# Output products, weight sums and bank copies moved around at the boundary between two layers

## The chip, the cores and the metric

The kernel runs on one core of a Trainium2 chip. The metric is the time of one execution in microseconds; the time before is the median of three runs.

## What is computed

Rotary attention on 2 x 8 heads of 576 tokens, then two feed-forward layers on the 1152 token rows, all with results to float32 accuracy (products run as pairs of hi and lo halves):

```python
attn = softmax(rotate(q) @ rotate(k).T / 8) @ v          # 16 heads, 576 x 64
x = attn as [1152, 512]
h = x @ w_in;   g = where(h > 0, h, exp(h) - 1);  x = g @ w_out    # 512 -> 2048 -> 512
h = x @ w2_in;  g = h * tanh(softplus(h));        out = g @ w2_out # 512 -> 2048 -> 512
```

## The kernel before

Every engine has one queue that it works through in order. Inside a `manual_schedule` block (L1311 to L1335) the order of the program is the order of each queue, so the code is the schedule.

A float32 matrix is split into a hi half (rounded by ScalarE) and a lo half (the rest, a subtract on VectorE or GpSimd), and a product takes three passes: hi by hi, hi by lo, lo by hi. Raw weights come from memory by DMA on SP's queue into three rotating buffers; ScalarE converts them (`rebase`, L92), VectorE restores their bits in three passes (`bits`, L103, L107, L111), after which the raw buffer is free for the next DMA, and `round_weight` makes the halves: hi on ScalarE (L116), lo on GpSimd or, where `by` says so, on VectorE (L117).

The first layer ends with four times `g2_mm` (TensorE, L922), `g2_y` (the sum into Y on VectorE, L936, and XH on ScalarE, L938) and `g2_xl` (XL on VectorE, L942). XH and XL hold the halves of the second layer's input.

The second layer (`second`, L1255) treats its 16 column blocks of 128 in eight pairs. Pair 0 is done plainly: three classic units (`classic`, L207 on TensorE, one for each 384 tokens), each followed by the Mish activation (`classic_act`, L1103), the hi half (`classic_hi`, L1106) and the lo half (`classic_lo`, L1110). Pairs 1 to 7 use Strassen-Winograd's scheme with seven products (`Pair.mm`, L1044) on 288-column blocks instead of eight. It wants sums of the inputs, t1 to t4 (`form`, L886 on VectorE; `put_hi`, L909 on ScalarE; `put_lo`, L913 on VectorE), and of the weights (`Pieces.sums`, L820 on VectorE; `Pieces.round`). t1's halves are written into XH and XL in place of the input block that they replace. The products accumulate in three PSUM banks of results, a, b and c; between products `copy` (L1064, ScalarE), `add` (L1068) and `add22` (L1072, VectorE) take partial results out, and `act` (L1082, L1083) and `lo` (L1086) make the activations' halves in a tile gg.

The output of a pair is nine products, one for each 128 tokens: `out_mm` (L1122, six matmuls on TensorE, into one of two banks ps_h) and `out_sum`, which for pair 0 copies the bank to Y (L1130, VectorE) and for later pairs adds it (L1132). In the step of pair q (`pair_step`, L1136) TensorE interleaves the seven products of pair q with the nine output products of pair q - 1, while the weights of pair q + 1 (`Pieces`) and the output weights of pair q (`Block`) are prepared. `ahead_pieces` are the weights of pair 1, which the first layer's last units load.

Of the kernel before, what the change touches and what calls it, by code (L numbers as in the profile page):

```python
# [13 lines left out]
AF = mybir.ActivationFunctionType  # L14
# [11 lines left out]
def kernel(  # L26
# [11 lines left out]
    nc = tc.nc  # L38
# [4 lines left out]
    NT, DM = out.shape  # L43
# [807 lines left out]
    def moe(mp, early):  # L851
# [46 lines left out]
        def put_hi(u, name):  # L898
            if name == "t1":
                home = x_home(top, u, 1)  # L900
            else:
                if u == 0 and name != "t4":
                    t = main.tile([128, 2, 2 * CH], F32R, tag="ge", name="ge", bufs=GE)[:, :, 0:2 * H2]
                else:
                    t = second_pool[0].tile([128, 2, 2 * H2], F32R, name=f"x{name}{u}")
                v = t.rearrange("p i (c n) -> p i c n", c=2)
                home = v[:, 0], v[:, 1]
            XO[u][name] = home
            nc.scalar.activation(out=home[0], in_=T[u][name], func=AF.Copy)  # L909

        def put_lo(u, name):
            hi, lo = XO[u][name]
            nc.vector.tensor_tensor(out=lo, in0=T[u][name], in1=plain(hi), op=ALU.subtract)  # L913
# [30 lines left out]
        def g2_first(g, t, ep):  # L944
            g2_y(g, t, ep, g2_mm(g, t, ep))
            if g == NG - 1:
                g2_xl(t, ep)

        UB = GF // 2
        pend = []  # L950
# [3 lines left out]
        ahead_pieces = Pieces(1)  # L954
# [171 lines left out]
        def out_sum():  # L1126
            pair, t, o = banks.pop(0)
            y = Y.rearrange("p (t e) -> p t e", e=DM)[:, t, :]
            if pair.q == 0:
                nc.vector.tensor_copy(out=y, in_=o)  # L1130
            else:
                nc.vector.tensor_tensor(out=y, in0=y, in1=o, op=ALU.add)  # L1132
                if pair.q == NF // 2 - 1:
                    nc.sync.dma_start(out=out[t * 128:t * 128 + 128, :], in_=y)

        def pair_step(x, prev, w, o, on):  # L1136
            x.mm(1)
# [117 lines left out]
        def second():  # L1255
            NQ = NF // 2
            x = Pair(0)
            w = ahead_pieces
            x.classic(0)
            w.round(0)  # L1260
            put_hi(0, "t4")
            form(1, "t3")
            form(1, "t2")
            x.classic_act(0)
            x.classic_hi(0)
            x.classic(1)
            w.sums(0, 1, 2)
            w.round(2)
            put_hi(1, "t2")
            x.classic_lo(0)  # L1270
            put_lo(1, "t2")
            x.classic_act(1)
            x.classic_hi(1)
            w.sums(3)
            form(0, "t1")
            form(1, "t1")
            put_hi(1, "t3")
            x.classic(2)
            x.classic_lo(1)
            w.round(1)  # L1280
            put_lo(1, "t3")
            form(1, "t4")
            put_lo(0, "t4")
            w.round(3)
            x.classic_act(2)
            x.classic_hi(2)
            put_hi(0, "t1")
            put_hi(1, "t1")
            put_lo(0, "t1")
            put_lo(1, "t1")  # L1290
            put_hi(1, "t4")
            o = [Block(NF + 2 + j) for j in range(2)]
            for b in o:
                b.load()
            put_lo(1, "t4")
            for q in range(1, NQ):
                prev, x = x, Pair(q)
                queue.extend((prev, t) for t in range(NT // 128))
                if q + 1 < NQ:
                    on = [Block(NF + 2 * q + 2 + j) for j in range(2)]  # L1300
                    pair_step(x, prev, Pieces(q + 1), o, on)
                    o = on
                else:
                    last_step(x, prev, o)
            queue.extend((x, t) for t in range(NT // 128))
            while queue:
                out_mm()
                out_sum()

        psum("ps_g")  # L1310
        with tc.manual_schedule():  # L1311
            for n in range(len(units)):
                step(n)
            (_, g, t, ep), = pend[:1]
            pend.pop(0)
            g2_first(g, t, ep)
            warm = mp.tile([128, 1], F32, name="warm")
            nc.gpsimd.memset(warm, 0.0)
            nc.scalar.activation(out=warm, in_=warm, func=AF.Mish)
            form(0, "t3")  # L1320
            form(0, "t2")
            form(0, "t4")
            put_hi(0, "t3")
            put_hi(0, "t2")
            o = [(x[1:], g2_mm(*x[1:])) for x in pend[:1]]
            g2_y(*o[0][0], o[0][1])
            put_lo(0, "t3")
            put_lo(0, "t2")
            g2_xl(*o[0][0][1:])
            g2_first(*pend[1][1:])  # L1330
            firsts.close()
            with tc.tile_pool(name="mp2", bufs=1, reuse_waits="tile") as mp2:
                second_pool[0] = mp2
                psum("ps_h")
                second()  # L1335
# [90 lines left out]
```

## Times and profile before

| | us |
|---|---|
| median of 3 runs | 553.16 (552.18 to 553.47) |
| the profiled execution, its own time | 551.88 |
| its span, first to last instruction | 550.1 |
| TensorE busy | 537.2 |
| VectorE busy | 431.4 |
| ScalarE busy | 310.0 |
| GpSimd busy | 233.4 |
| mean granted TensorE clock | 0.999 of 2.4 GHz |

The rows below come from the profiled execution. PE is TensorE, DVE VectorE, ACT ScalarE, POOL GpSimd, SPq SP's queue. A timeline row is start in us, duration in us, engine, line, operation, output<-input by the program's names, shape and count; in brackets stands how long the engine was idle before it and what ended that idle time. Rows of a timeline that follow each other on one engine may overlap by a tenth.

### The profile page before, as it was taken

The page shows a single profiled execution, that of the slowest core. Times are in us where ns is not written, and L with a number is a line of the kernel's source. Part 1 is how long each engine was busy: PE and PEld are TensorE (multiplying, and loading weights), DVE is VectorE, ACT ScalarE, POOL GpSimd, SP SyncE. Part 2 cuts the span into 40 slices and gives each one's busy share as a digit, 9 for nine tenths or more (in the row PEclk, how much of TensorE's full clock was granted, in tenths as well). Part 3 has the DMA queues.
Part 4 walks back from the last instruction along what each step waited for, and adds up shares of the span by engine and source line. Part 5 has one row for each costly group of instructions (what it writes and reads, how often), then busy time and mean ns, then how long its engine had stood idle before and what let it go on. Part 6 is the DMA issues. An engine that isn't in the chain of part 4 may idle for free.

```text
span 550.1 us, 9065 instructions
## 1 busy us (share of the span) xinstructions
PE 537.2 (98%) x3390; PEld 488.2 (89%) x3390; DVE 431.4 (78%) x671; ACT 310.0 (56%) x548; POOL 233.4 (42%) x207
## 2 busy tenths in 40 slices
PE   7999999999999999999999999979999999999997
PEld 6678887888899999999999999978889899888985
DVE  4667776788877987988888768899788888878853
ACT  3657676678556666455455554565654645556420
POOL 6899998843415442544344211132423313141200
PEclk9999999999999999999999999999999999999999
DMA  8278878874322333223232221104132231421004
GB/s 249 95 194 222 197 212 222 207 168 122 120 86 77 116 116 113 78 82 110 77 115 77 77 77 39 39 0 154 46 108 77 76 120 35 153 75 41 1 0 173
DMA packets 49100, 59.81 MB, mean 109 GB/s; under 512 B 20768, under 2 KB 38944, under 8 KB 48288
## 3 DMA queue, kind: packets, MB, share of 16 engines
q1 hardware_dynamic: 48512, 58.64, 36.4%
q8 instruction: 27, 0.44, 0.3%
q10 hardware_dynamic: 544, 0.59, 0.3%
q14 instruction: 17, 0.14, 0.1%
HBM read 47.51 MB, written 2.36 MB: 91 GB/s over the span
## 4 chain that ended last, share of the span: by engine, by line
PE 80%; DVE 9%; ACT 3%; POOL 3%; issue 2%; DMA 2%; SPq 0%; ACTq 0%; POOLq 0%; DVEq 0%
PE ps_h L1122 18%; PE ps_s L207 17%; PE ps_g L922 14%; PE ps_s L1044 13%; PE ps_s L441 7%; PE psA L548 6%; PE psT L508 4%; DMA tab<-in_rope_dram 1%; DVE Y L936 1%; DVE gg L886 1%; DVE mn L448 1%; DVE wu L111 1%; ACT XH L938 1%; DVE XL L942 1%; DMA qb<-ql 1%
## 5 line engine op out<-in xcount | busy, mean ns | idle before, releaser
L448 DVE TENSOR_REDUCE mn<-ps_s 128x1 f32<-128x576 f32 x72 | 53.7, 754 | 25.0 <-PE ps_s L441 24.9
L1132 DVE TENSOR_TENSOR Y<-Y,ps_h 128x512 f32<-128x512 f32 x63 | 43.2, 686 | 27.8 <-PE ps_h L1122 27.5
L461 ACT ACTIVATE P<-ps_s,mn 128x576 f32<-128x576 f32 x72 | 53.0, 737 | 14.4 <-DVE mn L448 14.1
L1122 PE MATMUL ps_h<-wo0h,gg 128*128 128x512 f32 x144 | 45.3, 396 | 0.6 <-DVE Y L1130 0.6
L1122 PE MATMUL ps_h<-wo0bh,gg 128*128 128x512 f32 x144 | 45.2, 395 | 0.0
L1064 ACT ACTIVATE ta<-ps_s 128x576 f32<-128x576 f32 x28 | 18.3, 652 | 46.3 <-PE ps_s L1044 46.3
L508 PE MATMUL psT<-idn,P 128*128 128x128 f32 x288 | 43.0, 274 | 0.0
L107 DVE SCALAR_TENSOR_TENSOR wu<-raw,wu 128x512 int32<-128x512 int32 x50 | 40.2, 805 | 1.4
L117 POOL TENSOR_TENSOR wo0l<-wu,wo0h 128x512 fp32r<-128x512 f32 x12 | 17.5, 1469 | 50.8 <-ACT wo0h L116 50.8
L528 ACT ACTIVATE pt<-psT 128x512 f32<-128x512 f32 x43 | 25.5, 594 | 22.7 <-PE psT L508 22.6
L111 DVE SCALAR_TENSOR_TENSOR wu<-raw,wu 128x512 int32<-128x512 int32 x50 | 36.2, 724 | 1.5
L254 DVE SCALAR_TENSOR_TENSOR tb<-ta,tb 128x768 f32<-128x768 f32 x22 | 21.4, 975 | 20.2 <-ACT tb L250 20.1
L117 POOL TENSOR_TENSOR wo0bl<-wu,wo0bh 128x512 fp32r<-128x512 f32 x12 | 17.1, 1443 | 46.5 <-ACT wo0bh L116 40.3
L548 PE MATMUL psA<-pt,v_t 128*64 128x256 f32 (+1 forms) x240 | 36.1, 401 | 0.6 <-ACT R L493 0.3
L508 PEld LDWEIGHTS psT<-idn,P 128*128 128x128 f32 x288 | 34.7, 141 | 1.9 <-issue 1.5
L103 DVE TENSOR_SCALAR wu<-wu 128x512 int32<-128x512 int32 x50 | 31.9, 649 | 0.0
L1122 PEld LDWEIGHTS ps_h<-wo0h,gg 128*128 128x128 f32 x144 | 26.0, 188 | 6.0 <-DVE Y L1130 1.0
L1122 PEld LDWEIGHTS ps_h<-wo0bh,gg 128*128 128x128 f32 x144 | 26.4, 188 | 5.5
L207 PE MATMUL ps_s<-XH,wi0h 128*128 128x384 f32 x120 | 31.0, 338 | 0.0
L207 PE MATMUL ps_s<-XL,wi0h 128*128 128x384 f32 x120 | 30.6, 335 | 0.0
L207 PE MATMUL ps_s<-XH,wi0l 128*128 128x384 f32 x120 | 30.5, 335 | 0.0
L117 POOL TENSOR_TENSOR wi0l<-wu,wi0h 128x512 fp32r<-128x512 f32 x10 | 14.9, 1493 | 35.7 <-ACT wi0h L116 35.7
(229 smaller groups left out, 1622.8 us busy)
## 6 DMA issues: line engine op xcount, KB each, us to landing
raw<-in_w_in_dram SPq DMA_DIRECT2D x32, 512.0 KB, 3.7
raw<-in_w_out_dram SPq DMA_DIRECT2D x32, 512.0 KB, 3.3
qk_t<-in_qk_dram SPq DMA_DIRECT2D x6, 1152.0 KB, 5.4
qa<-qh SPq DMA_DIRECT2D x24, 144.0 KB, 3.4
out_dram<-Y SPq DMA_DIRECT2D x9, 256.0 KB, 2.0
ka<-kh SPq DMA_DIRECT2D x12, 144.0 KB, 5.4
ka<-kl SPq DMA_DIRECT2D x12, 144.0 KB, 5.0
qb<-ql SPq DMA_DIRECT2D x12, 144.0 KB, 3.3
```

The source lines that it names most:

```text
L107: nc.vector.scalar_tensor_tensor(out=ui, in0=high, scalar=-0x80000000, in1=ui, op0=ALU.bitwise_and, op1=ALU.bitwise_or)
L111: nc.vector.scalar_tensor_tensor(out=ui, in0=low, scalar=29, in1=ui, op0=ALU.logical_shift_right, op1=ALU.bitwise_or)
L117: (by or nc.gpsimd).tensor_tensor(out=lo, in0=u, in1=plain(hi), op=ALU.subtract)
L207: nc.tensor.matmul(o[:, j, :CH], lhsT=ws[j][i][:, cc, :], rhs=x[:, cc, t * CH:t * CH + CH], start=(k == 0), stop=(k == 3 * NC - 1),)
L448: nc.vector.tensor_reduce(out=m, in_=psS[u][:, :, :HS], axis=AX.XY, op=ALU.min)
L461: nc.scalar.activation(out=P.rearrange("p (j n) -> p j n", j=2), in_=psS.pop(u)[:, :, :HS], func=AF.Exp, scale=-1.0, bias=mn_t.pop(u), acc ...
L508: nc.tensor.transpose(tv[:, c, :], P[:, k:k + 128], idn)
L548: nc.tensor.matmul(o[64 * h:64 * h + 64, cols], lhsT=v, rhs=rhs, start=(c == 0 and first), stop=(c == 4), skip_group_check=True,)
L922: nc.tensor.matmul(o[:, j, :CH], lhsT=WO[f][w][:, e * 128:e * 128 + 128], rhs=g_part(f, t, i), start=(k == 0), stop=(k == 3 * GF - 1),)
L1044: nc.tensor.matmul(self.o[r][:, u, :H2], lhsT=w[i][:, cc, :], rhs=XO[u][xn][x][:, cc, :], start=(first and n == 0), stop=(last and n == 3 ...
L1122: nc.tensor.matmul(o, lhsT=l, rhs=w, start=(k == 0), stop=(k == 5))
L1132: nc.vector.tensor_tensor(out=y, in0=y, in1=o, op=ALU.add)
```

## The change

`out_sum` of pair 0 goes from VectorE to ScalarE. The step of pair 1 has its own function, `first_step`. Three of its nine output products are issued in `second`, between the classic units and the first pair product, together with three sums. Around these, `second` is put in another order: `w.round`, `form` and the halves come in another sequence, and t4 of the second half of the tokens is formed in `first_step`. The four weight sums go from `second` to the end of the first layer, in between `g2_y` and `g2_xl`, and the first weight rounding and the load of the Mish table come ahead of them. In `first_step` the lo halves of the second output block and of three of the four weight roundings are subtracted on VectorE (in `pair_step`: of one).

```diff
--- before.py
+++ after.py
@@ -1127,11 +1127,75 @@
             pair, t, o = banks.pop(0)
             y = Y.rearrange("p (t e) -> p t e", e=DM)[:, t, :]
             if pair.q == 0:
-                nc.vector.tensor_copy(out=y, in_=o)
+                nc.scalar.activation(out=y, in_=o, func=AF.Copy)
             else:
                 nc.vector.tensor_tensor(out=y, in0=y, in1=o, op=ALU.add)
                 if pair.q == NF // 2 - 1:
                     nc.sync.dma_start(out=out[t * 128:t * 128 + 128, :], in_=y)
+
+        def first_step(x, prev, w, o, on):
+            o[0].bits(0)
+            x.mm(1)
+            x.copy("m1", "a")
+            o[0].bits(1)
+            x.mm(2)
+            o[0].bits(2)
+            o[0].round()
+            w.load(0)
+            form(1, "t4")
+            put_hi(1, "t4")
+            put_lo(1, "t4")
+            x.mm(6)
+            x.copy("u2", "a")
+            x.add("m1", "b")
+            x.mm(5)
+            x.mm(7)
+            out_mm()
+            o[1].bits(0)
+            out_mm()
+            x.copy("m5", "c")
+            x.act("m1")
+            w.bits(0, 0)
+            out_mm()
+            w.load(1)
+            out_mm()
+            o[1].bits(1)
+            x.copy("u3", "a")
+            x.mm(4)
+            o[1].bits(2)
+            x.add22()
+            out_sum()
+            w.bits(1, 0)
+            w.bits(0, 1)
+            w.bits(0, 2)
+            w.bits(1, 1)
+            out_mm()
+            out_sum()
+            o[1].round(nc.vector)
+            out_sum()
+            x.mm(3)
+            x.act("u3")
+            w.bits(1, 2)
+            out_sum()
+            w.sums(0)
+            out_mm()
+            w.sums(1)
+            on[0].load()
+            w.sums(2)
+            w.sums(3)
+            x.act("s")
+            x.lo("u3")
+            w.round(2, nc.vector)
+            x.add("u2", "c")
+            x.lo("m1")
+            w.round(0)
+            w.round(3, nc.vector)
+            on[1].load()
+            w.round(1, nc.vector)
+            x.act("u2")
+            out_sum()
+            out_sum()
+            x.lo("u2")
 
         def pair_step(x, prev, w, o, on):
             x.mm(1)
@@ -1256,49 +1320,52 @@
             NQ = NF // 2
             x = Pair(0)
             w = ahead_pieces
+            queue.extend((x, t) for t in range(NT // 128))
             x.classic(0)
-            w.round(0)
-            put_hi(0, "t4")
+            x.classic_act(0)
             form(1, "t3")
             form(1, "t2")
-            x.classic_act(0)
             x.classic_hi(0)
             x.classic(1)
-            w.sums(0, 1, 2)
             w.round(2)
+            put_hi(0, "t4")
+            x.classic_lo(0)
             put_hi(1, "t2")
-            x.classic_lo(0)
             put_lo(1, "t2")
+            w.round(1)
+            form(0, "t1")
+            form(1, "t1")
             x.classic_act(1)
             x.classic_hi(1)
-            w.sums(3)
-            form(0, "t1")
-            form(1, "t1")
+            put_lo(0, "t4")
+            x.classic(2)
+            w.round(3)
             put_hi(1, "t3")
-            x.classic(2)
             x.classic_lo(1)
-            w.round(1)
             put_lo(1, "t3")
-            form(1, "t4")
-            put_lo(0, "t4")
-            w.round(3)
-            x.classic_act(2)
-            x.classic_hi(2)
-            put_hi(0, "t1")
-            put_hi(1, "t1")
-            put_lo(0, "t1")
-            put_lo(1, "t1")
-            put_hi(1, "t4")
             o = [Block(NF + 2 + j) for j in range(2)]
             for b in o:
                 b.load()
-            put_lo(1, "t4")
+            out_mm()
+            out_mm()
+            put_hi(0, "t1")
+            put_hi(1, "t1")
+            x.classic_act(2)
+            out_sum()
+            x.classic_hi(2)
+            out_mm()
+            out_sum()
+            put_lo(0, "t1")
+            put_lo(1, "t1")
+            x.classic_lo(2)
+            out_sum()
             for q in range(1, NQ):
                 prev, x = x, Pair(q)
-                queue.extend((prev, t) for t in range(NT // 128))
+                if q > 1:
+                    queue.extend((prev, t) for t in range(NT // 128))
                 if q + 1 < NQ:
                     on = [Block(NF + 2 * q + 2 + j) for j in range(2)]
-                    pair_step(x, prev, Pieces(q + 1), o, on)
+                    (pair_step if q > 1 else first_step)(x, prev, Pieces(q + 1), o, on)
                     o = on
                 else:
                     last_step(x, prev, o)
@@ -1313,10 +1380,14 @@
                 step(n)
             (_, g, t, ep), = pend[:1]
             pend.pop(0)
-            g2_first(g, t, ep)
+            w = ahead_pieces
             warm = mp.tile([128, 1], F32, name="warm")
             nc.gpsimd.memset(warm, 0.0)
             nc.scalar.activation(out=warm, in_=warm, func=AF.Mish)
+            w.round(0)
+            g2_y(g, t, ep, g2_mm(g, t, ep))
+            w.sums(0, 1)
+            g2_xl(t, ep)
             form(0, "t3")
             form(0, "t2")
             form(0, "t4")
@@ -1327,7 +1398,10 @@
             put_lo(0, "t3")
             put_lo(0, "t2")
             g2_xl(*o[0][0][1:])
-            g2_first(*pend[1][1:])
+            g, t, ep = pend[1][1:]
+            g2_y(g, t, ep, g2_mm(g, t, ep))
+            w.sums(2, 3)
+            g2_xl(t, ep)
             firsts.close()
             with tc.tile_pool(name="mp2", bufs=1, reuse_waits="tile") as mp2:
                 second_pool[0] = mp2
```

## Rows read from the trace of the kernel before

**Rows 1.** The page: busy us (share of the span), instructions.
```profile
PE 537.2 (98%) x3390; PEld 488.2 (89%) x3390; DVE 431.4 (78%) x671; ACT 310.0 (56%) x548; POOL 233.4 (42%) x207
```

**Rows 2.** Waits of TensorE after 150 us: total, times, longest.
```profile
PE ps_s L1044 <- ACT ta L1064: 3.3, 1, 3.3
PE ps_h L1122 <- DVE Y L1130: 0.6, 1, 0.6
```

**Rows 3.** Stretches: length, busy us (instructions) by engine, clock, DMA share, GB/s.
```profile
363.17:391.23 28.06, 24.23 (x139) 21.21 (x139) 25.23 (x39) 18.02 (x30) 9.54 (x7) 1.00 0.24 76
391.23:414.96 23.73, 23.73 (x140) 21.27 (x139) 19.43 (x34) 13.11 (x22) 6.85 (x6) 1.00 0.28 89
414.96:438.60 23.64, 23.64 (x139) 21.23 (x138) 19.33 (x34) 13.13 (x22) 6.75 (x6) 1.00 0.28 89
```

**Rows 4.** Timeline, TensorE: start, us, instruction, idle before and its releaser.
```profile
363.17 0.42 PE L1044 MATMUL ps_s<-XH,wi1h 128*128 128x288 f32 x2
...
369.75 0.40 PE L1044 MATMUL ps_s<-ge,wi1h 128*128 128x288 f32 x1 [3.26 <-ACT ta L1064]
...
371.44 0.63 PE L1122 MATMUL ps_h<-wo0h,gg 128*128 128x512 f32 x2
...
372.84 0.63 PE L1122 MATMUL ps_h<-wo0h,gg 128*128 128x512 f32 x2
```

**Rows 5.** Timeline, ScalarE.
```profile
345.42 0.85 ACT L938 ACTIVATE XH<-Y 128x768 fp32r<-128x768 f32 x1 [3.36 <-DVE Y L936]
...
346.28 1.28 ACT L1319 ACT_TABLE_LOAD   x1
...
355.32 0.79 ACT L1103 ACTIVATE ta<-ps_s 128x768 f32<-128x768 f32 x1
...
367.36 0.68 ACT L909 ACTIVATE xt<-gg 128x576 fp32r<-128x576 f32 x1 [1.15 <-DVE gg L886]
...
367.95 1.21 ACT L92 ACTIVATE wu<-raw 128x512 f32<-128x512 f32 x2
...
369.06 0.63 ACT L1064 ACTIVATE ta<-ps_s 128x576 f32<-128x576 f32 x1
...
371.64 0.65 ACT L1064 ACTIVATE ta<-ps_s 128x576 f32<-128x576 f32 x1 [1.94 <-PE ps_s L1044]
```

**Rows 6.** Timeline, VectorE and, at 354.92, GpSimd.
```profile
346.30 0.96 DVE L942 TENSOR_TENSOR XL<-Y,XH 128x768 fp32r<-128x768 f32 x1 [0.92 <-ACT XH L938]
...
354.92 1.55 POOL L117 TENSOR_TENSOR wi1l<-wv,wi1h 128x512 fp32r<-128x512 f32 x1 [18.52 <-ACT wi1h L116]
...
355.23 1.85 DVE L886 TENSOR_TENSOR gg<-Y 128x576 f32<-128x576 f32 x1
...
357.80 0.42 DVE L820 TENSOR_TENSOR ws<-wv 128x256 f32<-128x256 f32 x1
...
366.58 0.74 DVE L886 TENSOR_TENSOR gg<-Y,gg 128x576 f32<-128x576 f32 x1
...
373.63 0.69 DVE L111 SCALAR_TENSOR_TENSOR wu<-raw,wu 128x512 int32<-128x512 int32 x1
```

**Rows 7.** Groups by line, ScalarE: busy us, mean ns, idle before.
```profile
L528 ACT ACTIVATE pt<-psT 128x512 f32<-128x512 f32 x43 | 25.5, 594 | 22.7 <-PE psT L508 22.6
...
L1083 ACT ACTIVATE gg<-ta 128x576 fp32r<-128x576 f32 x21 | 14.4, 688 | 0.7
...
L92 ACT ACTIVATE wv<-raw 128x512 f32<-128x512 f32 x14 | 9.3, 666 | 5.3 <-DMA raw<-in_w_in_dram 5.3
...
L116 ACT ACTIVATE wi1h<-wv 128x512 fp32r<-128x512 f32 x8 | 4.9, 616 | 0.0
```

**Rows 8.** One line each, L1130, L117, L78: ns or us, min/median/max.
```profile
L1130 DVE COPY Y<-ps_h x9: 678/690/690, 374.2 to 391.4; 128x512 f32<-128x512 f32 x9
...
L117 POOL TENSOR_TENSOR wi1l<-wu,wi1h x8: 1287/1414/2077, 175.6 to 275.2; 128x512 fp32r<-128x512 f32 x8
...
DMA to landing us min/median/max: 3.6/3.7/7.5
```

## The prediction, made before the changed kernel was run

> **What bounds the kernel.** I read the shares of the engines first. TensorE is busy for 537.2 of 550.1 us [rows 1], so time comes back only where TensorE stands still. Next come TensorE's own waits after 150 us. There are two, 3.3 us for ScalarE's copy at L1064 and 0.6 us for VectorE's copy at L1130 [rows 2], both in the first pair step of the second layer. The table by stretch shows what they are worth: from the end of the classic units to the next step's first product this step takes 28.06 us, while the next two, with the same nine output products and seven pair products, take 23.73 and 23.64 [rows 3]. **The most that this change can return is therefore 28.06 - 23.73 = 4.33 us.**
>
> Why TensorE waits is read from the queues. Pair product 6 starts at 369.75 [rows 4] because bank a must be copied first. That copy is issued at 369.06, behind the hi half of the last input sum t4, which waits 1.15 us for VectorE, and behind two conversions of raw weights [rows 5]. VectorE forms t4 only at 366.58 [rows 6]: it is busy 25.23 of the 28.06 us [rows 3]. The second wait is for the first of VectorE's copies of an output bank; there are two such banks, and the third product needs it.
>
> **The change, part by part.**
>
> *Three output products ahead of the pair products.* Nothing is added. An output product takes 372.84 - 371.44 = 1.40 us [rows 4], and a pair product (23.73 - 9 x 1.40) / 7 = 1.59. The classic units end at 363.17 [rows 4], so without a wait the order is: outputs 1 to 3 at 363.17, 364.57, 365.97; pair products 1, 2, 6, 5, 7 at 367.4, 369.0, 370.5, 372.1, 373.7; outputs 4 to 7 from 375.3; pair product 4 at 380.9; output 8; pair product 3 at 383.9; output 9; the next step at 386.9. What could keep TensorE from this order is costed next.
>
> *The nine first sums on ScalarE.* VectorE loses nine copies of 0.69 us [rows 8], 6.2 us. ScalarE gains nine. No row shows this copy there; the nearest are its 128x512 copy out of PSUM at 0.594 [rows 7] and a 128x768 activation out of PSUM at 0.79 [rows 5]. I take 0.59, the same shape and type, and keep 0.79 as the upper end; being the shape itself, it leaves no reason for less. By the rows ScalarE is the quicker of the two for this copy. A rule of the Trainium skill speaks against this part: "ScalarE: Activation LUTs", Rules for kernel authors, sends simple elementwise work to VectorE, at up to about three times ScalarE's speed in bf16. By that page a sum would cost some 2 us (an estimate: three times 0.69), which is the case of rival C.
>
> *Weight sums in the first layer.* Two of the four VectorE passes go into the wait for ScalarE ahead of L942 at 346.30, 0.92 us [rows 6], and two into the like wait ahead of the last L942. A pass takes 0.42 [rows 6], so two fill 0.84. The first two share their place with the GpSimd subtract of the first rounding, so I add up to 0.2 us; classic 1, which waits for it, begins only when classic 0 is done, about 355 [rows 5], and hides it. Without that cover it costs 0.2.
>
> *Table load earlier, t4 later.* The load, 1.28 us, moves into a wait of 3.36 us at 345.42 [rows 5] and costs nothing; without that wait it costs 1.28. t4 is used last by pair product 4, at 380.9, and is ready about 372.
>
> *Subtracts.* Three move from GpSimd to VectorE at 0.69 [rows 6], 2.1 us more. In return fewer collide: beside a GpSimd subtract begun at 354.92 a VectorE pass took 1.85 us, the like pass alone 0.74 [rows 6]. VectorE's balance in this step is 25.2 - 6.2 + 2.1 = 21.1 us, under 23.7.
>
> *Walk through ScalarE's queue*, with the durations of [rows 5, 7], less the 0.1 by which neighbours overlap (two conversions take 1.21), a TensorE result being read 0.2 us after the next product's start (371.64 against 371.44 [rows 4, 5]). Classic 0 is activated at about 355.1. To 362.9 follow its hi half, three roundings, three input sums' hi halves, classic 1, and the two raw conversions. The hi halves of both t1 follow to 364.1; the second overwrites inputs of classic 2 and must wait until 363.4 anyway. Then classic 2's activation to 364.8 and sum 1 to 365.4. **Output 3 wants it at 365.97: cover 0.5.** Bank a is copied from 369.2 to 369.8, 0.7 ahead of pair product 6; the second copy ends at 373.0, 0.7 ahead of pair product 7. Then m5's copy, two activations of m1, a conversion and u3's copy bring sum 4 to 377.5, 0.5 ahead of output 6, and sum 5 to 378.9, 0.5 ahead of output 7. The step's end is the fullest place: pair product 3 ends at 385.6, VectorE adds u2 to 386.4, ScalarE does two activations, sums 8 and 9, and the next step's first copy to 389.4, wanted at 390.0.
>
> *VectorE.* Ahead of output 3 its last duty is the second t1: from 355.4 there are six passes, 4.7 us, and two GpSimd subtracts of 1.4 [rows 8] may hold it, so 362.9 at the latest, 0.5 before it is needed. In the next step its eleven passes from the u2 sum to the raw bits take from 386.4 to about 392.9; the output bank that it reads next is ready at 393.2, and TensorE loses time only if VectorE is more than 0.7 late there.
>
> *DMA.* The loads keep their order on SP's queue. The second weight piece is fetched once the first block's bits are done, now about 369.1, and lands 3.7 us later [rows 8], at 373; it is converted at 375.8. The next two have 3.0 and 1.9 us of cover. The worst landing, 7.5 us, would put the first 0.8 us late, 0.5 of it covered.
>
> **Sum.** All covers hold by the rows, though six of them are only 0.5 to 0.7 us. The gain is 4.33, less 0.1 for what one of these may leak: 4.2 us. After this step TensorE has no wait [rows 2], so the gain reaches the end whole: the span goes from 550.1 to 545.9. The profiled execution took 551.88, its span and 1.8 around it, and lies 1.3 below the median of 553.16. The forecast is 553.16 - 4.2 = 549.0. Its own range, with a gain of 3.8 to 4.4 and the 1 us by which medians can move, is 548.0 to 550.0.
>
> **Rivals.** *A, part of the gain leaks through the thin covers.* A GpSimd subtract has reached 2.08 us, against a median of 1.41 [rows 8]. With two such ahead of the second t1, sum 1 comes 0.8 to 1.3 late and TensorE loses 0.3 to 0.8 there; the like lateness in VectorE's string at the next step costs another 1 to 2. For it: VectorE has hardly a gap in this step [rows 3]. Against: the median would not do it. A gain of 1.1 to 3.8, about 2.5: 550.7.
>
> *B, the wait only changes its name.* A raw weight that lands late, or dependences by whole tiles, takes the place of the old 3.3 us. For it: the conversion of weight pieces waits 5.3 us in all for its DMA [rows 7]. Against: on this path it would need a landing near 11 us; and pair product 1 starts at 363.17 [rows 4] although the t1 halves, which precede it in the program and go into the tile it reads, are written after it, so dependences go by regions. About 553.
>
> *C, slower: ScalarE becomes the bound.* With nine sums it is busy some 22 of 23.7 us. Up to the next step's first copy it still idles 4.7 us in the walk, always for a TensorE result (0.8 before sum 3, 1.0, 0.85 and 0.95 before the copies of m1, u2 and m5, 0.8 and 0.3 before sums 5 and 6). The sums may grow by 4.7 / 9 = 0.5 each before that is used up; each further 0.1 costs 0.9, so the gain of 4.3 is gone at 0.59 + 0.5 + 0.5 = 1.6 us a sum, and at 2.0 the kernel is 3.6 us slower: 556.8. For it: one queue holds the bank copies, the sums and the activations in a fixed order. Against: no ScalarE pass in the rows, up to 768 columns, takes over 0.85.
>
> **Chances.** Forecast 0.64, A 0.23, B 0.07, C 0.06. The range reaches over most of A, and below by the spread of the three runs (552.18 to 553.47): 547.5 to 551.5. Faster by over 0.2% (1.1 us, about what a measurement of this kernel can tell from no change) has forecast and A, 0.87; within 0.2% B, 0.07; slower C, 0.06.
>
> **What would show it.** The stretch from the end of the classic units to the next step's first matmul should read 23.7 to 24.1 instead of 28.06, with no TensorE wait above 0.3. A sum on ScalarE should take 0.59, the six covers should stand in the order above, and nothing on TensorE should wait for t4. A TensorE wait at output 3, 6 or 7 for a sum, or a copy at L1064 much later than 0.2 us after its product, makes A right; a wait for a DMA in this step's conversions makes B right; a ScalarE without gaps from 363 to 389, and sums far over 0.6, C. The prediction is wrong at its root if the stretch is short and the span is not: then later steps give the time back.

## The result and the profile after

The changed kernel takes 547.08 us (median of four executions, 547.00 to 547.33), the kernel before 553.32 beside it (four, 552.18 to 553.94): ratio 0.989, interval 0.9873 to 0.9907. It is faster by 6.2 us, where 4.2 was forecast, and the time lies 0.4 below the lower end of the range. Those four executions of before lie high: against the 60 further ones used below (median 552.55) the change is worth 5.5.

The profiled execution took 547.04, its span is 545.3, its mean granted clock 1.0. The page's shares of the engines answer to [rows 1]:

```profile
PE 536.4 (98%) x3390; PEld 488.3 (90%) x3390; DVE 426.8 (78%) x665; ACT 314.3 (58%) x557; POOL 229.2 (42%) x204
```

TensorE's work is the same; what is gone from the span is standing still. The boundary step by stretches (length, busy us by engine with instructions, clock, DMA share, GB/s), which answers to the first line of [rows 3]:

```profile
362.68:386.39 23.71, 23.71 (x139) 21.27 (x139) 18.13 (x31) 18.79 (x33) 2.59 (x2) 1.00 0.27 89
```

The step now takes 23.71 us, as long as the two steps behind it did before, and TensorE is busy in all of it. Its list of waits has no line behind 150 us, where [rows 2] had two. The waits that are left, over the whole span (total, times, longest), are all in the attention; the three longest groups:

```profile
PE ps_s L441 <- ACT P L461: 1.9, 4, 0.7
PE psA L612 <- DVE bl L596: 1.5, 1, 1.5
PE ps_s L441 <- DVE kh L323: 0.6, 1, 0.6
```

The places where TensorE could have waited, by its timeline (start, us, instruction), answering to [rows 4]: output 1, output 3, pair product 6, pair product 7, outputs 6 and 7, the next step's first product and its product 6.

```profile
362.68 0.63 PE L1122 MATMUL ps_h<-wo0h,gg 128*128 128x512 f32 x2
...
365.47 0.63 PE L1122 MATMUL ps_h<-wo0h,gg 128*128 128x512 f32 x2
...
370.03 0.29 PE L1044 MATMUL ps_s<-ge,wi1h 128*128 128x288 f32 x1
...
373.22 0.29 PE L1044 MATMUL ps_s<-ge,wi1h 128*128 128x288 f32 x1
...
377.61 0.63 PE L1122 MATMUL ps_h<-wo0h,gg 128*128 128x512 f32 x2
...
379.00 0.63 PE L1122 MATMUL ps_h<-wo0h,gg 128*128 128x512 f32 x2
...
386.39 0.42 PE L1044 MATMUL ps_s<-XH,wi0h 128*128 128x288 f32 x2
...
389.56 0.29 PE L1044 MATMUL ps_s<-ge,wi0h 128*128 128x288 f32 x1
```

None has a bracket. What each of them needs, by ScalarE's timeline (answering to [rows 5]):

```profile
364.27 0.60 ACT L1130 ACTIVATE Y<-ps_h 128x512 f32<-128x512 f32 x1
...
368.65 0.65 ACT L1064 ACTIVATE ta<-ps_s 128x576 f32<-128x576 f32 x1 [0.98 <-PE ps_s L1044]
...
371.82 0.65 ACT L1064 ACTIVATE ta<-ps_s 128x576 f32<-128x576 f32 x1 [0.88 <-PE ps_s L1044]
...
376.40 0.60 ACT L1130 ACTIVATE Y<-ps_h 128x512 f32<-128x512 f32 x1
377.81 0.60 ACT L1130 ACTIVATE Y<-ps_h 128x512 f32<-128x512 f32 x1 [0.80 <-PE ps_h L1122]
...
388.25 0.66 ACT L1064 ACTIVATE ta<-ps_s 128x576 f32<-128x576 f32 x1
```

Start plus duration against the start in TensorE's rows gives the six covers:

| what | ends | wanted | cover | cover forecast |
|---|---|---|---|---|
| sum 1, output 3 | 364.87 | 365.47 | 0.60 | 0.5 |
| copy of m1, product 6 | 369.30 | 370.03 | 0.73 | 0.7 |
| copy of u2, product 7 | 372.47 | 373.22 | 0.75 | 0.7 |
| sum 4, output 6 | 377.00 | 377.61 | 0.61 | 0.5 |
| sum 5, output 7 | 378.41 | 379.00 | 0.59 | 0.5 |
| next step's copy, its product 6 | 388.91 | 389.56 | 0.65 | 0.6 |

So the step did what the walk said, to a tenth. The 2 us by which the forecast missed must lie elsewhere. The difference of the two profiled executions is 551.88 - 547.04 = 4.84: 28.06 - 23.71 = 4.35 in the step, and 0.49 because the classic units end at 362.68 instead of 363.17 [rows 4]. The 0.49 is not the change's doing. It is there at the first layer's first matmul, some 200 us ahead of the first instruction that was moved (the kernel before, then the changed one):

```profile
145.46 0.62 PE L207 MATMUL ps_s<-XH,wi0h 128*128 128x384 f32 x2
```

```profile
144.93 0.62 PE L207 MATMUL ps_s<-XH,wi0h 128*128 128x384 f32 x2
```

From there to the end of the classic units pass 217.71 and 217.75 us, and 217.69 to 217.77 in all fourteen traces of this case. The earlier start comes out of the attention, where nothing was changed, and the moves at the end of the first layer gain nothing ahead of the step. The medians are 6.1 to 6.2 apart. What is left, some 1.3 us, is in no part of the profiled execution of before.

### The profile page after: what moved, and what is told of

It is laid out like the page before. It is cut to its first block, busy times and chain, and to the rows that moved or that the text cites. A ratio compares the mean times of both kernels' runs of the same rounds, so it can differ in the third digit from the quotient of the medians.

```text
span 545.3 us, 9059 instructions
## 1 busy us (share of the span) xinstructions
PE 536.4 (98%) x3390; PEld 488.3 (90%) x3390; DVE 426.8 (78%) x665; ACT 314.3 (58%) x557; POOL 229.2 (42%) x204
## 4 chain that ended last, share of the span: by engine, by line
PE 91%; POOL 3%; DMA 2%; DVE 2%; ACT 1%; issue 1%; SPq 0%; ACTq 0%; POOLq 0%; DVEq 0%
PE ps_s L207 21%; PE ps_h L1122 18%; PE ps_g L922 18%; PE ps_s L1044 14%; PE ps_s L441 7%; PE psA L548 6%; PE psT L508 4%; DMA tab<-in_rope_dram 1%; DMA raw<-in_w_in_dram 1%; DVE mn L448 1%; ACT P L461 1%; PE psT L548 1%; POOL qk_t L323 1%; POOL qk_t L320 1%; POOL qk_t L318 1%
## 5 line engine op out<-in xcount | busy, mean ns | idle before, releaser
L117 POOL TENSOR_TENSOR wo0l<-wu,wo0h 128x512 fp32r<-128x512 f32 x12 | 17.5, 1471 | 51.7 <-ACT wo0h L116 51.7
L117 POOL TENSOR_TENSOR wo0bl<-wu,wo0bh 128x512 fp32r<-128x512 f32 x11 | 15.5, 1419 | 46.7 <-ACT wo0bh L116 40.4
L117 POOL TENSOR_TENSOR wi0l<-wu,wi0h 128x512 fp32r<-128x512 f32 x10 | 14.9, 1492 | 35.6 <-ACT wi0h L116 35.6
```

The source lines that it names most:

```text
L117: (by or nc.gpsimd).tensor_tensor(out=lo, in0=u, in1=plain(hi), op=ALU.subtract)
```

## The experiments

### Where the 1.3 us lie

Each execution lists its mean granted clock. The changed kernel shows 0.998 to 1.0 in all eight of its executions (four above, four below). Of before, 60 executions with a clock were made beside the experiments:

| mean clock of before | executions | median us | range |
|---|---|---|---|
| 0.998 to 0.999 | 8 | 551.65 | 550.93 to 551.91 |
| 0.996 to 0.997 | 35 | 552.49 | 551.78 to 554.28 |
| 0.995 and less | 17 | 553.58 | 553.08 to 556.27 |
| all | 60 | 552.55 | 550.93 to 556.27 |

The execution that the prediction read was at 0.999, one of the few. **Theory (clock):** the hole of 3.3 us ahead of pair product 6 makes TensorE's clock fall in most executions, the matmuls behind the hole run at half speed for a while, and the change removes that as well as the hole. **Rival (start):** the clock is a sign of something else, the extra time lies in the attention or is chance, and the hole costs no more than its length. The most direct test is to profile before again (these three runs are the last in time).

> The kernel before, once more, for a trace of an ordinary execution: of 34 executions so far 27 have a mean granted clock of 0.994 to 0.997 and 7 of 0.999, as the profiled one has. Clock theory: this trace shows the clock at its lower level, half, for 3 to 4 us directly behind the 3.3 us wait at pair product 6, and nowhere else; the matmuls in that piece take longer, and the boundary step takes 28.9 to 29.9 instead of 28.06 us. Rival (the low mean comes from the attention part): the step takes 28.06 us and the clock is low before 160 us.

552.93 us (ten executions, 551.63 to 553.64). Its profiled execution, 551.63, was again at 0.999 and shows the step at 28.11: that decided nothing. Twice more, one execution each:

> The kernel before again, for a trace of an execution with a low mean clock; the last one read 0.999, as 7 of 57 executions do. The same two expectations hold. Clock theory: half clock for 3 to 4 us directly behind the wait at pair product 6, nowhere else, and a boundary step of 28.9 to 29.9 us. Rival: the low clock lies before 160 us and the step takes 28.06.

552.54 us, clock 0.997. TensorE's timeline of this execution behind the hole:

```profile
369.73 0.40 PE L1044 MATMUL ps_s<-ge,wi1h 128*128 128x288 f32 x1 [3.26 <-ACT ta L1064]
369.96 0.29 PE L1044 MATMUL ps_s<-xt,wi1h 128*128 128x288 f32 x1
370.10 0.29 PE L1044 MATMUL ps_s<-ge,wi1h 128*128 128x288 f32 x1
370.23 0.39 PE L1044 MATMUL ps_s<-xt,wi1h 128*128 128x288 f32 x1
370.42 0.44 PE L1044 MATMUL ps_s<-ge,wi1l 128*128 128x288 f32 x1
370.65 0.44 PE L1044 MATMUL ps_s<-xt,wi1l 128*128 128x288 f32 x1
...
372.33 1.05 PE L1122 MATMUL ps_h<-wo0h,gg 128*128 128x512 f32 x2
...
374.35 0.62 PE L1122 MATMUL ps_h<-wo0h,gg 128*128 128x512 f32 x2
```

The hole is the one of [rows 4], 3.26 us, and the second to the fourth matmul behind it start 0.13 to 0.14 us apart. The eight from 370.42 to 372.33 take 0.24 each, and the first output's pair of matmuls takes 1.05 us where [rows 4] has 0.63. The clock by stretches (the number ahead of the last two):

```profile
370.00:372.00 2.00, 2.00 (x11) 2.00 (x11) 1.97 (x4) 0.00 (x0) 0.00 (x0) 0.57 0.00 0
372.00:374.00 2.00, 2.00 (x8) 1.67 (x7) 1.93 (x4) 1.43 (x3) 0.18 (x1) 0.58 0.00 0
374.00:376.00 2.00, 2.00 (x11) 1.60 (x10) 1.05 (x3) 0.93 (x2) 2.00 (x2) 1.00 0.79 234
```

TensorE ran at 1.2 GHz for most of 370 to 374, and at 2.4 again from there. The same stretches of the execution that the prediction rests on show 1.00:

```profile
370.00:372.00 2.00, 2.00 (x15) 1.91 (x15) 1.97 (x5) 0.36 (x1) 0.00 (x0) 1.00 0.00 0
372.00:374.00 2.00, 2.00 (x10) 1.60 (x9) 1.93 (x4) 1.27 (x3) 0.26 (x1) 1.00 0.00 0
```

The Trainium skill, "TensorE: Matmul & The Clock Gate", Part 1, says that the engine's clock passes only every second pulse when it has been idle. By the same part matmuls in this state start their columns divided by 1.2 GHz apart, for 288 columns 0.24 us, an estimate from that rule. The rows agree, 0.24.

By the clock column 2 x 0.43 + 2 x 0.42 = 1.70 us of work are lost. By the rows it is 1.53: from product 6 to the second output pass 374.35 - 369.73 = 4.62 us, in [rows 4] 372.84 - 369.75 = 3.09. The second wait of [rows 2] vanishes in exchange, because VectorE's first output copy is no longer late for a slower TensorE: the list of waits of this execution has one line behind 150 us.

```profile
PE ps_s L1044 <- ACT ta L1064: 3.3, 1, 3.3
```

That wait of 0.57 had cost the step 0.84 (why more than 0.57, the last section shows). So the step is longer by 1.53 - 0.84 = 0.69 only: 28.75 us (363.14 to 391.89) against 28.06, a little under the 28.9 that the clock theory had as its least.

> As before_third, in case that one reads 0.999 as well; where both are low, one of 0.994 should show the lower level for about 6.6 us (twice that of 0.997) in the same place.

551.83 us, clock 0.997. The same wait of 3.26, and a fall that begins earlier; the step takes 28.61, again under 28.9.

```profile
369.20:371.00 1.80, 1.80 (x7) 1.80 (x8) 1.76 (x5) 0.00 (x0) 0.00 (x0) 0.50 0.00 0
371.00:373.00 2.00, 2.00 (x10) 1.86 (x10) 1.96 (x3) 0.57 (x2) 0.00 (x0) 0.69 0.00 0
373.00:375.00 2.00, 2.00 (x10) 1.62 (x9) 1.38 (x2) 1.67 (x4) 1.32 (x2) 1.00 0.57 158
```

Both 0.997 executions have the fall directly behind the hole and nowhere else in the span, where the rival puts nothing. No execution of before at 0.995 or less was profiled, so where its further 1.1 us lie stays open.

Next, before with its hole filled: twelve matmuls into a bank that nobody reads.

```diff
             x.mm(1)
             x.mm(2)
+            if x.q == 1:
+                d = g_pool[0].tile([128, 512], F32, tag="h", name="ps_h", bufs=2)
+                for _ in range(12):
+                    nc.tensor.matmul(d, lhsT=XH[:, 2, 0:128], rhs=XH[:, 2, 0:512], start=True, stop=True)
             prev.last_lo()
```

> The kernel before, with twelve matmuls added between pair products 2 and 6 of the first pair step; their result is read by nobody. They fill 12 x 0.233 = 2.8 us of the 3.4 us hole on TensorE and move nothing else. The changed kernel gained 6.2 us by the medians, but only 4.35 in the boundary step and 0.4 by an earlier start in its trace; some 1.5 us are not explained. Theory 1 (clock): in most executions of the kernel before, the hole makes TensorE's granted clock fall for a while, which the one profiled execution of 551.88 us does not show. Then this kernel takes 551.6 to 552.0 in every execution, some 1.4 below the median of the kernel before beside it, with a small spread. Theory 2 (start): the 1.5 us come from the attention part, where executions differ by chance; then this kernel has the median and the spread of the kernel before, 553.2, within 0.3.

551.79 us (twelve executions, 551.34 to 555.21) against 552.49 of before beside it (23): ratio 0.9988, interval 0.9971 to 1.0006. The clock is 0.998 to 1.0 in eleven of the twelve; the twelfth, at 0.996, is the one of 555.21. In the trace the hole is 0.54 us:

```profile
367.45 2.90 PE L1142 MATMUL ps_h<-XH 128*128 128x512 f32 x12
370.90 0.40 PE L1044 MATMUL ps_s<-ge,wi1h 128*128 128x288 f32 x1 [0.54 <-ACT ta L1064]
```

The gain is 0.7, half of the 1.4 expected, and by its interval alone it could be none. Most of the shortfall is the base: 553.16 lies 0.61 over the median of the 60 executions. The levels say more: 551.79 is where before lies when its clock stays up (551.65), and the step takes 28.10 as in those executions (28.06, 28.11). Added work that nobody needs made nothing slower, and the low clock is gone from eleven of twelve executions. The narrow spread that the clock theory expected, 551.6 to 552.0, did not come: five of the twelve lie in it. Its profiled execution, 553.04, is late by 1.1 us already where the first layer begins.

The converse, the changed kernel with a hole of its own: ten copies on ScalarE ahead of the copy of m1.

```diff
         def first_step(x, prev, w, o, on):
+            late = second_pool[0].tile([128, 512], F32, name="late")
             o[0].bits(0)
             x.mm(1)
+            for _ in range(10):
+                nc.scalar.activation(out=late, in_=Y[:, 0:512], func=AF.Copy)
             x.copy("m1", "a")
```

> The changed kernel with ten copies of 128x512 on ScalarE added ahead of the copy of m1, which nobody reads. They hold pair product 6 back and put a hole of about 3.4 us on TensorE at the place of the old one (ten times 0.52, less 0.8 that ScalarE idles there and 0.7 of cover, 3.3 to 3.7). Theory 1 (clock): 547.1 + 3.4 + 1.4 = 552, with the wide spread of the kernel before. Theory 2 (start): 547.1 + 3.4 = 550.5, with the narrow spread of the changed kernel.

553.64 us (twelve executions, 553.15 to 554.71), ratio to before 1.002 (1.0009 to 1.0031); the clock is 0.992 to 0.997 in all twelve. Three rows of the profiled execution, 553.52 us, on ScalarE and TensorE:

```profile
367.68 6.59 ACT L1141 ACTIVATE late<-Y 128x512 f32<-128x512 f32 x10
374.18 0.63 ACT L1064 ACTIVATE ta<-ps_s 128x576 f32<-128x576 f32 x1
```

```profile
374.86 0.40 PE L1044 MATMUL ps_s<-ge,wi1h 128*128 128x288 f32 x1 [4.55 <-ACT ta L1064]
```

The copies take 0.65 from one to the next (367.68 to 374.18 for ten), not 0.52, so that the hole is 4.55 us and not some 3.4. Product 6 starts 374.86 - 362.80 = 12.06 us into the step, in the changed kernel 370.03 - 362.68 = 7.35: it is 4.71 later, so the rival gives 547.1 + 4.7 = 551.8, and none of the twelve is below 553.15. The stretches behind it show the rest:

```profile
374.00:376.00 2.00, 1.14 (x6) 1.14 (x7) 0.00 (x0) 2.00 (x5) 0.60 (x1) 0.81 0.00 0
376.00:378.00 2.00, 2.00 (x10) 2.00 (x10) 1.49 (x3) 0.61 (x2) 0.69 (x1) 0.50 0.00 0
378.00:380.00 2.00, 2.00 (x15) 2.00 (x14) 1.93 (x4) 0.63 (x2) 0.00 (x0) 0.84 0.00 0
```

The step takes 30.07 (362.80 to 392.87), that is 23.71 + 4.71 + 1.65, and the sum 547.1 + 4.7 + 1.65 = 553.4 is what was measured to 0.2. Of the 1.65, 0.11 is the first matmul behind the hole, and 1.54 the low clock, as much as the 1.53 of the first trace at 0.997. The rival falls: a hole that was put in by hand brings the low clock, behind itself, with its price. Because it is longer than the hole of before, a shorter one was made too.

It is the same with `range(5)`:

> As gap_made, with five copies instead of ten ahead of the copy of m1. In gap_made ten copies took 6.6 us and left a hole of 4.55 us on TensorE, after which the clock stood at half for about 3.4 us. Five should take 3.3 and leave a hole of 1.6 us. Clock theory: a hole of this length leaves the clock at its upper level, the mean clock reads 0.998 to 1.0 in every execution, and the cost is the hole alone, 547.1 + 1.6 = 548.7, with a narrow spread. Rival (any hole pays a price of its own, about 1.4 us): 550.1 and a lower mean clock.

548.76 us (seven executions, 548.45 to 551.20), ratio 0.9942 (0.9924 to 0.9960); the clock is 0.999 to 1.0 in all seven.

```profile
374.09 0.40 PE L1044 MATMUL ps_s<-ge,wi1h 128*128 128x288 f32 x1 [1.25 <-ACT ta L1064]
```

This hole costs 25.24 - 23.71 = 1.53 in the step and 1.7 in the median, and no clock. A hole of 1.25 us had its clock up in 7 of 7 executions, one of 3.26 in 8 of 60, one of 4.55 in none of 12 (each length read from the traced executions, the clock from the mean of each).

### What each part of the change is worth

The changed kernel once more, so that the others have it beside them:

> The changed kernel again, in more executions beside the kernel before. Theory 1: 547.0 to 547.4, and 6.2 below the kernel before, on any chip. Theory 2: the distance to the kernel before changes from one set of executions to the next, between 4.4 and 6.5, and the changed kernel has slow starts too.

547.18 us (546.68 to 548.03), ratio 0.990 (0.9882 to 0.9919). Theory 1 did not hold in its distance: the 23 executions of before beside these have a median of 552.49, 5.3 above and not 6.2. That fits theory 2 as well, under which the distance changes from set to set; the 6.2 of the first comparison was in part chance. With the first four, the median of eight is 547.08. From here one part at a time is undone. The sums on VectorE again:

```diff
             if pair.q == 0:
-                nc.scalar.activation(out=y, in_=o, func=AF.Copy)
+                nc.vector.tensor_copy(out=y, in_=o)
```

> The changed kernel with the nine first sums back on VectorE. By the walk through the queues outputs 6 and 7 then wait behind VectorE's bits and t4's subtract, output 7 by about 1.7 us and output 6 by about 0.6, and the step ends 2.2 to 2.7 us later: 549.5. If the sums' engine did not matter (rival: all the gain is the three products' place) it stays at 547.1.

549.64 us (549.43 to 549.73), ratio 0.9943 (0.9922 to 0.9964). Waits for VectorE's copy of a bank, like the second of [rows 2], are back, at outputs 6 and 7, where the walk had them at 0.6 and 1.7:

```profile
378.25 0.73 PE L1122 MATMUL ps_h<-wo0h,gg 128*128 128x512 f32 x2 [0.26 <-DVE Y L1130]
...
381.12 0.73 PE L1122 MATMUL ps_h<-wo0h,gg 128*128 128x512 f32 x2 [1.20 <-DVE Y L1130]
```

The sum t4 formed and rounded ahead of the boundary again:

```diff
         def first_step(x, prev, w, o, on):
...
             w.load(0)
-            form(1, "t4")
-            put_hi(1, "t4")
-            put_lo(1, "t4")
             x.mm(6)
...
             put_lo(1, "t3")
+            form(1, "t4")
...
             put_hi(1, "t1")
+            put_hi(1, "t4")
             x.classic_act(2)
...
             x.classic_lo(2)
+            put_lo(1, "t4")
             out_sum()
```

> The changed kernel with the last input sum t4 back in front of the first products: formed behind t3's lo half on VectorE, its hi half on ScalarE ahead of classic 2's activation. Walk: VectorE forms it at 365 to 365.7, ScalarE waits for it, classic 2's activation and sum 1 come 1.7 late, output 3 waits for sum 1 and the whole step ends 1.7 later: 548.8, mean clock 0.998 to 1.0. Rival (t4's place does not matter once the products fill the hole): 547.1 to 547.3.

549.02 us (548.64 to 551.11), ratio 0.9936 (0.9912 to 0.9960). Sum 1 comes behind t4 in ScalarE's queue, and output 3 waits for it:

```profile
366.97 0.73 PE L1122 MATMUL ps_h<-wo0h,gg 128*128 128x512 f32 x2 [1.20 <-ACT Y L1130]
```

The three output products and their sums behind pair product 6 again:

```diff
         def first_step(x, prev, w, o, on):
...
             x.mm(6)
+            out_mm()
+            out_mm()
+            out_mm()
             x.copy("u2", "a")
+            out_sum()
+            out_sum()
+            out_sum()
             x.add("m1", "b")
```

(and the three `out_mm` and three `out_sum` in `second` taken out).

> The changed kernel with the three early output products and their sums back behind pair product 6, as in the kernel before; all else of the change stays, the sums on ScalarE too. Walk through the queues: t4 is out of the way of the copy of m1, so the old 3.3 us wait does not come back; instead output 3 waits about 1 us for sum 1, behind the copy of u2 on ScalarE, and the pair step ends 1.2 later: 548.3, mean clock at 0.998 to 1.0. Rival (the place of the three products is what the gain hangs on): the hole comes back, 551 to 552, mean clock 0.997.

547.93 us (547.79 to 548.57), ratio 0.9919 (0.9897 to 0.9942); the clock is 0.999 to 1.0.

```profile
371.00 0.73 PE L1122 MATMUL ps_h<-wo0h,gg 128*128 128x512 f32 x2 [0.54 <-ACT Y L1130]
```

The old hole does not return: with t4 gone from its way, the copy of m1 is no longer late even where the products don't stand ahead. The four weight sums in `second` again:

```diff
             x.classic_hi(0)
+            w.sums(0, 1, 2, 3)
             x.classic(1)
...
             g2_y(g, t, ep, g2_mm(g, t, ep))
-            w.sums(0, 1)
             g2_xl(t, ep)
...
             g2_y(g, t, ep, g2_mm(g, t, ep))
-            w.sums(2, 3)
             g2_xl(t, ep)
```

> The changed kernel with the four weight sums back in the second layer, behind classic 0's hi half. They put 1.7 us of VectorE work ahead of the second t1, which had 0.5 us of cover towards sum 1 and output 3, and part of it fills a wait of VectorE. Walk: output 3 starts 0.3 late, 547.4. Rival (VectorE has no slack there, each of the four passes shows): 548.3 to 548.8.

547.95 us (five executions, 547.53 to 549.95), ratio 0.9927 (0.9901 to 0.9953). The trace has a single wait at output 3, for sum 1, and a step of 24.20, 0.49 longer than the change's:

```profile
366.25 0.73 PE L1122 MATMUL ps_h<-wo0h,gg 128*128 128x512 f32 x2 [0.22 <-ACT Y L1130]
```

The remaining 0.4 of the median is not this part's: the profiled execution, which is the median one, ends its classic units at 363.07, 0.39 later than the changed kernel, and is that late at the first layer's first matmul already (145.37). The subtracts on GpSimd again:

```diff
-            o[1].round(nc.vector)
+            o[1].round()
...
-            w.round(2, nc.vector)
+            w.round(2)
...
-            w.round(1, nc.vector)
+            w.round(1)
```

> The changed kernel with the three subtracts of the first step (second output block, weight roundings 2 and 1) back on GpSimd. VectorE does 2.1 us less, but each subtract on GpSimd of 1.3 us can hold a VectorE pass with two inputs. Walk: nothing in the step itself, at most 0.4 at the next step's third output product: 547.1 to 547.5. Rival (the held passes add up, as rival A has it): 548.1 to 549.1, with TensorE waiting for VectorE's sums in the second pair step.

547.38 us (547.29 to 548.25), ratio 0.9911 (0.9887 to 0.9934); the clock is 0.999 to 1.0 but for the execution of 548.25, at 0.997. The step takes 23.71, and the list of TensorE's waits has no line behind 150 us. The walk was right nonetheless: the next step takes 24.09 us (386.26 to 410.35), 0.37 more than the 23.72 of the changed kernel, and its third output product begins 0.52 us after the last matmul of the second, where 0.23 is usual:

```profile
393.58 0.40 PE L1122 MATMUL ps_h<-wo0bl,gg 128*128 128x512 f32 x1
394.10 0.73 PE L1122 MATMUL ps_h<-wo0bh,gg 128*128 128x512 f32 x2
```

The wait shows in the page's line of the weight loads (last column), which has no such releaser in the changed kernel:

```profile
L1122 PEld LDWEIGHTS ps_h<-wo0bh,gg 128*128 128x128 f32 x144 | 26.3, 188 | 5.9 <-DVE Y L1132 0.6
```

VectorE is late there because passes beside GpSimd's subtracts are long again, two of them 1.48 and 1.51 us where the changed kernel has 0.75 and 0.42:

```profile
385.74 1.48 DVE L1086 TENSOR_TENSOR gg<-ta,gg 128x576 fp32r<-128x576 f32 x1
387.14 1.51 DVE L117 TENSOR_TENSOR wi0l<-ws,wi0h 128x256 fp32r<-128x256 f32 x1
```

So this part is worth about 0.4 us, too little for the medians to tell from nothing by themselves.

| undone | us | over the change's 547.08 | step us | over its 23.71 | next step, over its 23.72 |
|---|---|---|---|---|---|
| sums on ScalarE | 549.64 | 2.6 | 25.95 | 2.24 | 0.34 |
| t4 later | 549.02 | 1.9 | 25.18 | 1.47 | 0.00 |
| products ahead | 547.93 | 0.9 | 24.67 | 0.96 | 0.00 |
| weight sums earlier | 547.95 | 0.9 | 24.20 | 0.49 | 0.00 |
| subtracts on VectorE | 547.38 | 0.3 | 23.71 | 0.00 | 0.37 |

The two columns of steps add up to 5.87, more than the 4.35 that all of them bring. A likely reason, which was not tested, is that the parts shorten the same two queues, so that with one undone the others' covers are used up. The rest of the new order was not undone by itself: the first rounding and the table load ahead of their old places, and the sequence of pair products, copies and bits within `first_step`.

## Why the prediction was off, point by point

**The walk held.** The ceiling of 4.33 us was reached: 4.35. The covers are those forecast (table above). The weight sum beside the first rounding's GpSimd subtract took 0.67 us instead of 0.42, the 0.2 allowed and 0.05. A sum on ScalarE takes 0.59 us, as taken (nine of them, busy us, mean ns, idle before):

```profile
L1130 ACT ACTIVATE Y<-ps_h 128x512 f32<-128x512 f32 x9 | 5.2, 593 | 2.0 <-PE ps_h L1122 1.9
```

The rule in the Trainium skill's "ScalarE: Activation LUTs", Rules for kernel authors, speaks of bf16; for this float32 copy out of PSUM the measurement decides, 0.59 against VectorE's 0.69 [rows 8].

**Rival A** (a leak through thin covers) was wrong for this kernel: no cover was used up. The leak itself exists: with three subtracts back on GpSimd it showed as 0.37 us in the next step, one of the two places that the rival named. A GpSimd subtract, as it feared, did fall on the two passes of t1; they took 2.52 us, 1.0 more than twice the 0.74 of [rows 6], and ended at 358.94 + 2.52 = 361.46, well before the 362.9 allowed:

```profile
358.94 2.52 DVE L886 TENSOR_TENSOR gg<-Y 128x576 f32<-128x576 f32 x2
```

**Rival B** (the wait only changes its name) was wrong; no wait of TensorE is left behind 150 us, and the second weight piece, forecast to be converted at 375.8, was converted at 375.26 without a wait for its DMA. **Rival C** (ScalarE becomes the bound) was wrong: it is busy 18.79 of 23.71 us, not some 22. Its idle time up to the next step's first copy is 0.80 before sum 3, 0.98, 0.88 and 0.95 before the copies, 0.80 and 0.28 before sums 5 and 6, together 4.69, where the walk had 4.7. VectorE's balance was sized too high, 18.13 instead of 21.1: eight instructions fewer than in [rows 3] fall in the stretch, not six, and they take 0.58 us instead of 0.65 on average, with GpSimd busy for 2.59 us there instead of 9.54.

**The step that failed is the base**: "lies 1.3 below the median of 553.16. The forecast is 553.16 - 4.2 = 549.0". It carried the 1.3 us between the profiled execution and the median over to the changed kernel as if they belonged to every stretch alike. The runs place the larger part of them behind the hole or in chance: the median of all 60 executions lies 0.90 above that of the eight whose clock stayed up. TensorE at 1.2 GHz behind the hole is shown as a cause of this: it was seen in two traces, whose steps are 0.55 and 0.69 longer, came back with a hole made on purpose, and was gone from eleven of twelve executions where the hole was filled. What the executions at 0.995 and less lose beyond that was not traced. Removing the hole removes the low clock too, so that the saving in a usual execution is 4.35 + 0.90 = 5.25, not 4.2; the medians of 60 and eight executions are 5.47 apart. From the eight at high clock to the eight of after it is 551.65 - 547.08 = 4.57, the step and 0.2.

The miss of 549.0 - 547.08 = 1.92 is thus 0.15 from the step (4.35 for 4.2), 1.28 from the base, and 0.49 from a start that was earlier in the profiled execution of after. Of the 1.28, 0.90 is the distance of the usual execution from those at high clock; 0.61 is the median of three executions, 553.16, above that of 60; and -0.23 the profiled execution above its own group's median. The 0.61 and the 0.49 are luck. The classic units end between 362.57 and 363.17 in the four profiled executions of before, and between 362.55 and 363.07 in those of the changed kernel and its variants, but for two late starts (365.32 with the shorter hole, 364.29 with the hole of before filled). In every one of them the difference is there at the first layer's first matmul, so that it comes from the attention and not from the moves behind it.

The range failed by the same step. The forecast's own range was also added up wrongly: gains of 3.8 to 4.4 and 1 us either way give 547.8 to 550.4, not 548.0 to 550.0, and rival A's leaks of 1.3 to 2.8 give gains of 1.5 to 3.0, not 1.1 to 3.8. Below, the range as a whole reached only as far as the three runs spread, and no rival of the prediction was on the side of a greater gain: that a hole costs more than its length was not among them, although three executions spread over 1.3 us and a profiled one below them asked where they differ.

## What to carry to other kernels

When the profiled execution is faster than the median, look at the granted clock of each execution before setting a saving against either: a hole in TensorE's work may cost its length in the one that was profiled and more in the others. The length of a step against the same step later in the kernel told the gain to 0.02 us, better than the list of waits did (3.83 for 4.35); a walk of the queue that feeds it, cover by cover, told whether the gain is reached. Undo the parts one by one before crediting any of them: here the place of the products, the most visible part, was worth 1.0 us by the steps, ScalarE's sums and the later t4 2.6 and 1.5. Read the step behind as well: the subtracts' 0.37 us lay there alone. And before a difference is put down to a change, compare the times at a point ahead of it: here half a microsecond was there 200 us earlier.

## What the runs showed of the hardware

The clock behind a hole differs from execution to execution of one program: with a hole of 3.26 us the mean clock says that TensorE stayed at 2.4 GHz in 8 of 60 executions and not in the other 52. In the two of these that were traced it fell to 1.2 GHz at the end of the hole (0.50 from 369.2) or 0.6 us behind it (370.4), and the stretches from 373 and from 374 read 1.00 again. It delayed TensorE's matmuls by 1.53 and 1.38 us there and by 1.54 behind the made hole; in before the step grew by 0.69 and 0.55 only, since the slower matmuls hid the next wait, worth 0.84.

A wait in the list is shorter than the time that it costs. Single waits of 1.25, 1.20 and 0.22 us made their steps 1.53, 1.47 and 0.49 longer, and the two of before, 3.26 and 0.57, add up to 3.83 where the step lost 4.35: about 0.27 more each. The rows show where: the last matmul's end, drawn some 0.16 behind the start of what could have followed it (0.29 long at a spacing of 0.13), and the first matmul behind the wait, 0.40 long instead of 0.29 [rows 4]. So product 6 itself began 1.42 and 4.71 us later behind the holes of 1.25 and 4.55, 0.16 or 0.17 more than the list says. A pause can also cost time without any line in the list, as the 0.37 us of the subtracts did.

Ten copies on ScalarE into one tile took 6.59 us, 0.63 long and 0.65 from one to the next, where a copy of a bank into Y was 0.59 long and the instruction behind it began 0.49 after it (364.27 to 364.76); which of the two differences (the same tile written again, SBUF instead of PSUM read) makes it was not tried apart.
